# Three small early reads of x and of two weights into an unused buffer, in a kernel of cross attention and a gated MLP

## The chip, the cores and the metric

The kernel runs on one core of one Trainium2 chip. The metric is the device time in microseconds (us); the kernel before has a median of 220.04 us over 3 runs (219.81 to 221.09).

## What is computed

For each of 8 batches and 8 heads, x (512 tokens of 64 values) and a state (32 slots of 64 values) attend to each other. Both results, 544 rows per batch of 8 × 64 = 512 values, then go through a gated MLP with 1536 hidden values. Inputs and output are float32.

```
scores = scale * x @ state.T        a  = softmax(scores)    xread = a  @ state
scores2 = scale * state @ x.T       a2 = softmax(scores2)   sread = a2 @ x
t = concat([xread, sread], rows)    -> (B * 544, 512)
out = (relu(t @ w_gate) * (t @ w_val)) @ w_out
```

## The kernel before

The matrix products run in bf16. For the x rows the kernel does not build xread: it forms U = state · w (lines 291 to 320, for both weights), so that `gv` (line 338) needs only the normalised attention `ANS` as the other operand. `relu` on ScalarE (line 351) and `mult` on VectorE (line 356) make `h_sb`, and `out_part` (line 402) multiplies it with `w_out` into `o_ps`. The state rows are collected in `br` and go through the same weights at the end (`gvs`, line 343).

The order of the first third is written out by hand: the string `program` (lines 455 to 483) names every step, and each engine takes its instructions in that order. The steps that matter here:

- Ahead of the string, lines 414 to 420 issue the first loads without a cast: SP issues heads 0 and 1 of batch 0; ScalarE issues the state of batches 0 and 1 and then heads 2 and 3 of batch 0. They land in `st_f` and `xf`, and `stc` and `xc` cast them. Line 427 issues heads 4 to 7 of batch 0 from GpSimd, which casts in the transfer.
- `dx.1.0.2` and `dx.1.1.2` (line 434) load batch 1 in two halves. `dw.w.lo.n` (line 109) loads n columns of all 512 rows of a weight: 0 is gate, 1 is value. All these come from GpSimd's queue, one behind the other: four pieces of 128 columns, then ten of 256.
- `spin32` and `spin` (line 438) are matmuls of constants into an unused bank; they stand between the early steps and keep TensorE running.
- `xT` transposes x on TensorE and `xo` copies it out of PSUM; `sc` makes the scores, `ex` the exponentials, `nr` and `nx` the normalisation. `c` makes columns of U, `co` copies them, and `gv`, `re`, `mu` and `o` are the MLP.

x lies in memory as (batch, head, token, 64 values). One batch is 1 MB, one head 128 KB. A row of `w_gate` or `w_val` is 6 KB.

After these, SP issues transposes in the transfer (for example `ad.2`, line 226) and the output rows (line 379). The pool `const` is the first in the memory of a partition; behind it lie, in this order, the pools of `U`, `xf`, `xb` and the other attention tiles, small tiles, `ANS`, `h_sb`, `g_sb` and `o_sb`.

Of the kernel before, what the change touches and what calls it, by code (L numbers as in the profile page):

```python
# [8 lines left out]
FP32 = mybir.dt.float32  # L9
# [7 lines left out]
def kernel(  # L17
# [9 lines left out]
    nc = tc.nc  # L27
# [10 lines left out]
    def pool(name, bufs, space=None):  # L38
        if space is None:
            return ctx.enter_context(tc.tile_pool(name=name, bufs=bufs))  # L40
        return ctx.enter_context(tc.tile_pool(name=name, bufs=bufs, space=space))

    const = pool("const", 1)
# [53 lines left out]
    def state_dma(eng, lo, hi):  # L97
        src = state.rearrange("(g b) h (m i) d -> (b h m) g i d", b=2, i=4)
        eng.dma_start(out=st_f[:, lo // 2:hi // 2], in_=src[:, lo // 2:hi // 2])
# [312 lines left out]
    ctx.enter_context(tc.manual_schedule())  # L412
    nc.vector.memset(stT, 0.0)
    xf[0] = xin.tile([128, HK, NC, D], FP32, name="xf", tag="xf")
    for eng, j in ((nc.sync, 0), (nc.scalar, None), (nc.scalar, 1)):
        if j is None:
            state_dma(eng, 0, 2)
        else:
            src = x[0, 2 * j:2 * j + 2].rearrange("h (p c) d -> p h c d", c=NC)
            eng.dma_start(out=xf[0][:, 2 * j:2 * j + 2], in_=src)  # L420
    nc.scalar.activation(out=tiny, in_=nc.const_aps.tensor(0.0, (128, 1), FP32), func=AF.Exp)

    def w_load(w, lo, n):
# [130 lines left out]
    for g in range(first, NF * (B + 1)):  # L554
        b, jf = divmod(g, NF)
# [47 lines left out]
```

## Time and profile before

| | us |
|---|---|
| median of 3 runs | 220.04 |
| the profiled execution | 219.39 |
| its span, first to last instruction | 217.6 |
| TensorE busy (1952 matmuls) | 212.8 |
| VectorE busy | 135.0 |
| ScalarE busy | 117.8 |
| GpSimd busy | 42.5 |

The span is that of one profiled execution; 1.79 us of its 219.39 lie outside it. Matmuls overlap in the pipeline, so their durations add to more than the time they occupy. PE is the matmul part of TensorE and PEld its loading of the stationary operand; DVE is VectorE, ACT ScalarE, POOL GpSimd, SP SyncE; a q behind a name is the engine's issuing queue. In a row of the timeline the first number is the start in us from the span's start, the second the duration, and the bracket tells how long the engine was idle before and what ended that. The chain of waits follows the work that ended last back to its start. A row of the transfers gives the size and the time from the start of the issue to the landing. "DMA share" is the summed time of packets over 16 transfer engines and the length of the window: over 1 means that packets overlap on an engine. GB/s counts what is written; the casting loads read twice as many bytes as they write.

### The profile page before, as it was taken

Reading aid. Unit: us, or ns where it says so; the run is one execution under the profiler, and the core shown is the slowest. Engines: PE = TensorE matmul, PEld = TensorE weight load, DVE = VectorE, ACT = ScalarE, POOL = GpSimd, SP = SyncE. Lnnn points to the kernel's source line nnn. Section 1 sums busy time; section 2 is a strip of 40 time slices with the busy share of each in tenths; the row PEclk is TensorE's granted clock in tenths of the full one; section 3 lists DMA queues with packets and bytes.
Section 4 is the critical chain, followed back from the end, with each engine's and each line's share of the span. In section 5 each row is a group of like instructions: output and inputs, shape, how many; then the busy total and the mean of one; then the engine's idle time right before and its main releaser. Section 6 shows DMA issues by size and latency. Waiting matters only on the chain.

```text
span 217.6 us, 4865 instructions
## 1 busy us (share of the span) xinstructions
PE 212.8 (98%) x1952; PEld 104.8 (48%) x1952; DVE 135.0 (62%) x233; ACT 117.8 (54%) x225; POOL 42.5 (20%) x63
## 2 busy tenths in 40 slices
PE   8899999999999999999999999999999999999994
PEld 4554454454444444444444444444544445666543
DVE  4799967956887678557966796388745444222100
ACT  4798877747546556455555656454646443333221
POOL 7974049005600531020107000000000000000000
PEclk9999999999999999999999999999999999999999
DMA  7999999579963995919491453131311122222132
GB/s 168 180 196 197 202 221 171 78 139 188 152 175 74 144 186 110 167 52 193 99 148 60 110 134 96 49 99 50 84 28 51 48 48 50 61 56 80 51 96 96
DMA packets 47399, 24.96 MB, mean 115 GB/s; under 512 B 27824, under 2 KB 43056, under 8 KB 47376
## 3 DMA queue, kind: packets, MB, share of 16 engines
q0 software_dynamic: 16896, 9.05, 31.0%
q1 hardware_dynamic: 29584, 14.85, 28.7%
q10 hardware_dynamic: 896, 0.75, 1.3%
q8 instruction: 15, 0.25, 0.4%
q14 instruction: 8, 0.07, 0.2%
HBM read 18.35 MB, written 8.91 MB: 125 GB/s over the span
## 4 chain that ended last, share of the span: by engine, by line
PE 96%; DVE 1%; ACT 1%; issue 0%
PE o_ps L367 40%; PE gv_ps L325 38%; PE gv_ps L347 5%; PE up L298 4%; PE warm_ps L440 2%; PE upc L298 2%; PE o_ps L396 1%; PE sr_ps L265 1%; PE sc_ps L179 1%; PE sT_ps L189 1%; PE xT_ps L162 1%; ACT e_sn L206 1%; DVE xT L165 1%; ACT xT L165 0%; PE aT_ps L234 0%; DVE cs L212 0%
## 5 line engine op out<-in xcount | busy, mean ns | idle before, releaser
L367 PE MATMUL o_ps<-wo_sb,h_sb 128*128 128x512 bf16 x372 | 94.3, 379 | 0.0
L325 PE MATMUL gv_ps<-ans,U 128*128 128x512 bf16 x384 | 93.2, 379 | 0.0
L358 DVE TENSOR_TENSOR h_sb<-gv_ps,g_sb 128x512 bf16<-128x512 f32 x96 | 65.1, 688 | 42.8 <-ACT g_sb L354 41.3
L354 ACT ACTIVATE g_sb<-gv_ps 128x512 bf16<-128x512 f32 (+1 forms) x108 | 61.7, 578 | 51.4 <-PE gv_ps L325 39.1
L325 PEld LDWEIGHTS <-U 128*128 128x128 bf16 x384 | 37.1, 98 | 44.5 <-issue 0.8
L367 PEld LDWEIGHTS <-h_sb 128*128 128x128 bf16 x372 | 35.2, 98 | 42.0 <-issue 4.0
L310 DVE CAST U<-up 128x512 bf16<-128x512 f32 x44 | 27.7, 684 | 5.7 <-PE up L298 5.7
L375 ACT COPY o_sb<-o_ps 128x512 f32<-128x512 f32 x31 | 18.4, 594 | 19.7 <-PE o_ps L367 17.7
L310 ACT CAST U<-up 128x512 bf16<-128x512 f32 x28 | 14.7, 595 | 8.8 <-PE up L298 8.8
L254 POOL COPY xa<-xb 128x1024 bf16<-128x1024 bf16 x16 | 16.0, 1045 | 10.0 <-PE sr_ps L265 5.9
L358 DVE TENSOR_TENSOR hs_sb<-gv_ps,g_sb 128x256 bf16<-128x256 f32 x12 | 5.1, 425 | 15.3 <-PE gv_ps L347 10.4
L212 DVE TENSOR_REDUCE cs<-e_sn 128x16 f32<-128x512 bf16 x16 | 10.8, 677 | 1.1 <-ACT e_sn L206 1.1
L218 DVE TENSOR_TENSOR a_sn<-e_sn,rc 128x512 bf16<-128x512 bf16 x16 | 10.9, 687 | 0.4
L298 PEld LDWEIGHTS <-stT 64*32 64x32 bf16 x560 | 6.7, 91 | 6.4 <-issue 5.3
L320 ACT CAST U<-upc 128x512 bf16<-128x512 f32 (+1 forms) x19 | 8.7, 522 | 1.7 <-PE upc L298 1.7
L446 POOL COPY mark<-g_sb 128x1 bf16<-128x1 bf16 x4 | 0.8, 190 | 41.8 <-ACT g_sb L354 41.8
L197 ACT ACTIVATE eT<-sT_ps 128x512 bf16<-128x512 f32 x10 | 5.4, 594 | 5.3 <-PE sT_ps L189 5.3
L434 POOL DMA_DIRECT2D xb<-in_x_dram x8 | 6.8, 847 | 3.1 <-DMA wg_sb<-in_moe_w_gate_dram 1.4
L347 PE MATMUL gv_ps<-br,wg_sb 128*128 128x256 bf16 x48 | 7.2, 273 | 0.0
L347 PE MATMUL gv_ps<-br,wv_sb 128*128 128x256 bf16 x48 | 7.2, 273 | 0.0
L399 DVE COPY o_sb<-o_ps 128x64 f32<-128x64 f32 x2 | 0.4, 224 | 10.6 <-PE o_ps L396 10.5
L298 PE MATMUL up<-wg_sb,stT 64*32 64x512 bf16 (+1 forms) x168 | 6.9, 348 | 0.0
(59 smaller groups left out, 124.1 us busy)
## 6 DMA issues: line engine op xcount, KB each, us to landing
out_dram<-o_sb SPq DMA_DIRECT2D x26, 256.0 KB, 2.4
xb<-in_x_dram POOLq DMA_DIRECT2D x6, 512.0 KB, 7.1
wo_sb<-in_moe_w_out_dram POOLq DMA_DIRECT2D x2, 768.0 KB, 10.5
out_dram<-o_sb SPq DMA_DIRECT2D x11, 128.0 KB, 2.4
wg_sb<-in_moe_w_gate_dram POOLq DMA_DIRECT2D x5, 256.0 KB, 9.4
wv_sb<-in_moe_w_val_dram POOLq DMA_DIRECT2D x5, 256.0 KB, 10.0
xb<-in_x_dram POOLq DMA_DIRECT2D x3, 256.0 KB, 5.3
st_f<-in_state_dram POOLq DMA_DIRECT2D x1, 384.0 KB, 11.4
```

Of the source, the lines that this page charges most:

```text
L212: nc.vector.reduce_sum(out=cs, in_=e_v, axis=AX.X)
L218: {"dve": nc.vector, "pool": nc.gpsimd}[eng].tensor_tensor(out=a_sn[b][:, jp].rearrange("p c (j n) -> p c j n", n=Ns), in0=e_v, in1=held[" ...
L254: nc.gpsimd.tensor_copy(out=v[:, hs], in_=xb[b][:, hs])
L298: nc.tensor.matmul(dst[kc][i0:i0 + 32], stT[r:r + 64, parity, b, h], wsb[r:r + 64, j, lo:lo + n], start=True, stop=True)
L310: copy[eng](out=U[b][:, w, kc, lo:lo + 512], in_=held["u", b, w, lo][kc])
L320: copy[eng](out=U[b][:, :, kc, lo:lo + n], in_=held["c", b, lo][kc])
L325: nc.tensor.matmul(ps[w], U[b][:, w, kc, f0:f0 + 128], ANS[b][:, kc].rearrange("p c t -> p (c t)"), start=(kc == 0), stop=(kc == NK - 1))
L347: nc.tensor.matmul(ps[w][:, 0:nt], wsb[:, j, f0:f0 + 128], br[:, j].rearrange("p b n -> p (b n)"), start=(j == 0), stop=(j == NJ - 1))
L354: nc.scalar.activation(out=g_sb[:, 0:n], in_=ps[0][:, 0:n], func=AF.Relu)
L358: nc.vector.tensor_tensor(out=dst, in0=ps[1][:, 0:n], in1=held["g", b, jf][:, 0:n], op=ALU.mult)
L367: nc.tensor.matmul(held["o", b, tsub], src[:, jf, tsub * 128:(tsub + 1) * 128], wo_sb[:, jf], start=(jf == 0), stop=(jf == NF - 1))
L375: copy[eng](out=o_sb, in_=held["o", b, tsub])
```

## The change

Behind SP's first load (heads 0 and 1 of batch 0), and in the program's text behind ScalarE's two, SP issues three more. Each copies 32 bytes (8 float32) from the start of each of a row of equal stretches into a new tile `touch` in the pool `const`:

- of x: 96 pieces, one each 64 rows of 64 values (16 KB), from 512 KB to 2 MB, which is heads 4 to 7 of batch 0 and all of batch 1;
- of `w_gate` and of `w_val`: 32 pieces each, one each 16 rows (96 KB), over the whole weight.

Nothing reads `touch`. It takes 96 bytes of each partition at the end of `const`, so every tile of the later pools begins 96 bytes further on: `o_sb`, for example, at byte 212896 in place of 212800. Nothing else is edited, and the order on the other engines is as before.

```diff
     xf[0] = xin.tile([128, HK, NC, D], FP32, name="xf", tag="xf")
+    touch = const.tile([96, 3, 8], FP32, name="touch")
+
+    def touch_dma(k, src, lo, n, step):
+        v = src.rearrange("(a r) c -> a r c", r=step)[lo:lo + n, 0, 0:8]
+        nc.sync.dma_start(out=touch[0:n, k], in_=v)
+
     for eng, j in ((nc.sync, 0), (nc.scalar, None), (nc.scalar, 1)):
         if j is None:
             state_dma(eng, 0, 2)
         else:
             src = x[0, 2 * j:2 * j + 2].rearrange("h (p c) d -> p h c d", c=NC)
             eng.dma_start(out=xf[0][:, 2 * j:2 * j + 2], in_=src)
+    touch_dma(0, x.rearrange("b h s d -> (b h s) d"), 32, 96, 64)
+    touch_dma(1, moe_w_gate, 0, 32, 16)
+    touch_dma(2, moe_w_val, 0, 32, 16)
     nc.scalar.activation(out=tiny, in_=nc.const_aps.tensor(0.0, (128, 1), FP32), func=AF.Exp)
```

## The prediction

> **What bounds the kernel.** I read the page's busy times and slices first, then the chain of waits in order of time, then the timeline of the first 20 us beside the landings of single transfers, because the change touches only the first microseconds.
>
> ```profile
> span 217.6 us, 4865 instructions
> PE 212.8 (98%) x1952; PEld 104.8 (48%) x1952; DVE 135.0 (62%) x233; ACT 117.8 (54%) x225; POOL 42.5 (20%) x63
> ...
> DMA  7999999579963995919491453131311122222132
> ...
> PE 96%; DVE 1%; ACT 1%; issue 0%
> ```
>
> TensorE is busy 98% of the span and the chain of waits is 96% TensorE, with no transfer among its shares. The transfer engines are full in the first slices of 5.4 us each. So faster loads can help only in the opening, and only where TensorE or the chain waits for one. The chain there:
>
> ```profile
> 0.78 3.75 PE warm_ps L440 x4
> ...
> 5.17 0.44 PE xT_ps L162 x4
> ...
> 5.63 0.42 DVE xT L165
> ...
> 8.38 0.25 DVE rc L214
> ...
> 8.66 0.70 DVE xT L165
> ...
> 9.41 0.42 PE sc_ps L179 x8
> ...
> 15.91 2.70 PE gv_ps L325 x12
> 18.61 0.56 PE upc L298 x32
> ```
>
> It opens with 3.75 us of matmuls on constants, whose length no load sets. From 5.63 to about 12 us it runs through VectorE and ScalarE; from there TensorE works without a gap. Beside it stand these instructions and landings:
>
> ```profile
> 0.74 0.46 SPq L420 DMA_DIRECT2D xf<-in_x_dram  x1
> 1.19 0.45 ACTq L420 DMA_DIRECT2D xf<-in_x_dram  x1
> 2.67 1.50 POOL L434 DMA_DIRECT2D xb<-in_x_dram  x2
> 4.16 0.76 POOL L109 DMA_DIRECT2D wg_sb<-in_moe_w_gate_dram  x1
> 4.72 0.45 DVE L144 CAST xb<-xf 128x512 bf16<-128x512 f32 x1 [0.88 <-DMA xf<-in_x_dram]
> 4.89 0.77 POOL L109 DMA_DIRECT2D wv_sb<-in_moe_w_val_dram  x1
> 5.50 0.53 PE L162 MATMUL xT_ps<-id,xb 128*128 128x128 bf16 x4
> 5.62 0.78 POOL L109 DMA_DIRECT2D wg_sb<-in_moe_w_gate_dram  x1
> 6.35 0.79 POOL L109 DMA_DIRECT2D wv_sb<-in_moe_w_val_dram  x1
> 7.97 0.62 PE L162 MATMUL xT_ps<-id,xb 128*128 128x128 bf16 x8
> 9.54 0.74 POOL L109 DMA_DIRECT2D wv_sb<-in_moe_w_val_dram  x1 [0.18 <-issue]
> ```
>
> ```profile
> xf<-in_x_dram ACTq DMA_DIRECT2D x1, 256.0 KB, 3.5
> xb<-in_x_dram POOLq DMA_DIRECT2D x1, 256.0 KB, 5.2
> wg_sb<-in_moe_w_gate_dram POOLq DMA_DIRECT2D x1, 128.0 KB, 5.8
> wv_sb<-in_moe_w_val_dram POOLq DMA_DIRECT2D x1, 128.0 KB, 5.8
> wv_sb<-in_moe_w_val_dram POOLq DMA_DIRECT2D x1, 256.0 KB, 8.8
> ```
>
> The time to landing counts from the issue's start, so each load has a spare, the time by which it may be late before the chain moves:
>
> - Heads 2 and 3 of batch 0, from ScalarE's queue: 1.19 + 3.5 = 4.69. The cast ends at 4.72 + 0.45 = 5.17 and TensorE transposes at 5.50: spare 0.3 us.
> - First half of batch 1: 2.67 + 5.2 = 7.87. Its eight transposes run from 7.97 to 7.97 + 0.62 = 8.59, and VectorE, which copies them, is free at 8.38 + 0.25 = 8.63: **spare 0.04 us**, the smallest. Earlier arrival gains nothing: VectorE is the later of the two.
> - The fourth value piece: 9.54 + 8.8 = 18.34, first used by the `upc` at 18.61, to which TensorE comes without a gap: spare 0.25 us or so.
>
> **The change, part by part.** *Three issues on SP.* One issue of SP's takes 0.46 us (the row at 0.74), so they fill SP from 1.20 to about 2.6 us. What is queued behind them:
>
> ```profile
> SPq L226 <- DVE sn L274: 43.1, 1, 43.1
> ```
>
> SP then waits 43.1 us for VectorE before its next issue, so this costs nothing; without that cover it would be 3 × 0.46 = 1.4 us. Nobody waits for the new transfers. Each transfer on SP's and ScalarE's queues waits, for its counter, for the eighth transfer before it; three more shift which counter it is but not that distance, so I take nothing for it.
>
> *160 pieces on the transfer engines.* They are 96 + 32 + 32 reads of 32 bytes, 10 on each of 16 engines if spread evenly. They come behind SP's own load in its queue and meet ScalarE's load and the first casting loads of GpSimd. The trace has no 32-byte read. The nearest row is the 128-column weight pieces: 512 runs of 256 bytes written each, landing at 4.16 + 5.8 = 9.96 and 4.89 + 5.8 = 10.69. That is 0.73 us for 512 runs on full engines, so 160 runs hold the stream 0.73 × 160 / 512 = **0.23 us**. (GpSimd also issues them 0.73 us apart, so the engines alone may do them faster.) The ends of this term come from a queue's total and from an idle stretch:
>
> ```profile
> q0 software_dynamic: 16896, 9.05, 31.0%
> ```
>
> ```profile
> 2.00:3.00 1.00, 1.00 (x2) 0.43 (x2) 1.00 (x1) 0.99 (x2) 0.93 (x4) 1.00 0.79 223
> 8.00:9.00 1.00, 1.00 (x17) 0.78 (x17) 0.93 (x3) 0.62 (x3) 1.00 (x2) 1.00 1.60 171
> 9.00:10.00 1.00, 0.74 (x16) 0.59 (x16) 1.00 (x3) 0.72 (x2) 0.82 (x2) 1.00 1.81 178
> 10.00:11.00 1.00, 0.91 (x23) 0.44 (x20) 0.93 (x3) 1.00 (x2) 1.00 (x2) 1.00 1.82 179
> 12.00:13.00 1.00, 0.96 (x53) 0.59 (x50) 0.97 (x4) 1.00 (x3) 1.00 (x2) 1.00 1.45 195
> ```
>
> A packet of GpSimd's queue (q0) takes 31.0% × 16 × 217.6 us / 16896 = 64 ns. Ten of them without overlap are 0.64 us, the upper end. The lower end of the cost is 0: the share of 0.79 from 2 to 3 us leaves some engine time free, and the pieces may fall there.
>
> The Trainium skill speaks against the change here, in "DMA: Bandwidth & Descriptors", section "Measured (HBM→SBUF, 128 partitions, SWDGE, issued from GpSimd)": it puts the floor of a small transfer at about 10.5 ns for each packet. By that, an estimate, 160 pieces would hold the engines 1.7 us, and the sum below would be +1.6 in place of +0.2. The rows above show 512 runs in 0.73 us, 1.4 ns each, on full engines, so the trace does not bear this floor out for runs of 256 bytes; no run here shows it for 32.
>
> *What the reads may save.* If the first read of a stretch is slow, the loads behind the touches run faster. The window rows bound this: from 8 to 11 us, when new stretches of x and of both weights are first read, 171, 178 and 179 GB/s are written against 195 at 12 to 13 us. The deficit is 24 + 17 + 16 = 57 KB, and 57 KB / 195 GB/s = 0.29 us. Most of that I put to the 512-byte reads of the narrow pieces, because the second pair of narrow pieces, over the same rows, shows the same 0.73 us: issued at 5.62 and 6.35, with the same 5.8 us to landing. I take a saving of 0, with 0.29 us as its end.
>
> *What arrives late, and the sum.* The stream behind the touches is late by 0.23 us (−0.29 to +0.64). ScalarE's load eats that in its spare of 0.3. Batch 1's first half has 0.04: the copy at 8.66, the scores at 9.41 and all behind them move 0.23 − 0.04 = 0.19 us. The fourth value piece moves 0.23 against a TensorE that comes 0.19 later, inside its spare. TensorE is full from then on, so what is lost stays lost. Sum: 219.39 + 0.19 = 219.58 for the profiled execution. The median of the runs shown is 0.65 above that execution, so 220.04 + 0.19 = **220.2 us**.
>
> *The shift of 96 bytes* of every later tile costs nothing that a row shows. Only a slower matmul would move the end. I take 0.
>
> **The rivals.**
>
> 1. *Nothing was cold, and the pieces fit into idle engine time.* For it: share 0.79 from 2 to 3 us. Against: the share is 1 and above from 3 us on, and SP's own load stands ahead of the pieces. The time stays at 220.0.
> 2. *The loads land sooner, and that helps.* The end of the saving is 0.29 us. Against: no link of the chain is a transfer, and VectorE at 8.63 is later than the data. For it: timed runs are 0.65 us above the profiled one, so there a load may be the later. Then 220.04 − 0.29 = 219.75; with all 0.65 recovered, 219.4.
> 3. *The pieces themselves pay a slow first read, with engines held.* This one ends on the slow side, and its price comes from the first load against a late transfer of the same size:
>
> ```profile
> xf<-in_x_dram SPq DMA_DIRECT2D x1, 256.0 KB, 3.3
> ...
> out_dram<-o_sb SPq DMA_DIRECT2D x1, 256.0 KB, 2.0
> ```
>
>    The first took 1.3 us longer (part of that is other traffic, and one reads while the other writes). If one such wait holds the engines for all pieces together, the chain moves 1.3 − 0.04 = 1.26 us: 221.3. If each of the three transfers pays it, 3.9 − 0.04: 223.9. It passes 1% when the pieces hold the engines 2.2 us, 0.22 us for each of the ten on an engine. Against: 0.73 us for 512 first-read runs of a weight leaves no room for many such waits.
> 4. *The 96-byte shift slows reads.* The price is by the two large groups of matmuls:
>
> ```profile
> L367 PE MATMUL o_ps<-wo_sb,h_sb 128*128 128x512 bf16 x372 | 94.3, 379 | 0.0
> L325 PE MATMUL gv_ps<-ans,U 128*128 128x512 bf16 x384 | 93.2, 379 | 0.0
> ```
>
>    They are 756, so one nanosecond on each is 0.76 us, 220.8. Nothing in the trace speaks for it.
>
> **How the numbers follow.** My forecast, a small loss from the pieces (220.05 to 220.6), has 0.45; no change 0.22; a small gain 0.15; the slow first reads 0.12, a third of it with each transfer paying; the shift 0.06. The predicted time is that of the forecast, 220.2. The range goes from 219.4 (all of the saving in rival 2) to 221.3 (one slow wait in rival 3), which leaves out the 223.9 and some tails, under 2 in 10. The bound of 1%, 2.2 us, is about what a measurement of this kernel can tell from no change. No case gains 2.2 us, so faster gets 0.02 for what I have not seen; slower has the bad third of rival 3 and a little of rival 4, 0.06; within 1% is 0.92.
>
> **What would show it.** Right: SP's three issues between 1.2 and 2.6 us; the first half of batch 1 landing near 8.1 in place of 7.87; the copy of its transposes by VectorE near 8.85 in place of 8.66, waiting for TensorE; the matmuls at 18.61 near 18.8; everything later moved by as much. Rival 1 would show the same landing as now, rival 2 an earlier one and 9 to 11 us at 190 GB/s or more. Rival 3 would show landings late by 1 us and a gap on TensorE between 5.5 and 9 us. The shift would show in a mean matmul time above 379 ns. I am wrong if the landing moves by more than 0.64 us or if the time falls while the chain's opening stays as it is.

## The result

| | us | runs |
|---|---|---|
| before, median | 220.41 (219.51 to 221.92) | 22 |
| changed, median | 219.56 (219.00 to 220.94) | 22 |
| ratio | 0.9969, 95% interval 0.9956 to 0.9983 | |
| profiled execution, before / changed | 219.39 / 219.64 | |

The changed kernel is 0.31% faster, some 0.7 us by the ratio and 0.85 between the medians, where 0.19 us of loss was forecast. The time lies in the range of 219.4 to 221.3, and the sign is the other one. At the same time its profiled execution is slower than the profiled one of before. The page after:

```profile
span 217.8 us, 4845 instructions
PE 209.6 (96%) x1926; PEld 104.3 (48%) x1952; DVE 134.8 (62%) x233; ACT 117.9 (54%) x225; POOL 42.6 (20%) x63
```

TensorE's record count fell from 1952 to 1926 while its weight loads stand at 1952: matmul records are missing, so its 209.6 us are no gain. What the opening looks like, first the timeline of the changed kernel (start, duration, instruction):

```profile
1.25 0.45 SPq L419 DMA_DIRECT2D touch<-in_x_dram  x1
1.75 0.43 SPq L419 DMA_DIRECT2D touch<-in_moe_w_gate_dram  x1
2.22 0.42 SPq L419 DMA_DIRECT2D touch<-in_moe_w_val_dram  x1
8.41 0.62 PE L162 MATMUL xT_ps<-id,xb 128*128 128x128 bf16 x8 [0.30 <-DMA xb<-in_x_dram]
9.06 0.69 DVE L165 COPY xT<-xT_ps 128x1024 bf16<-128x1024 bf16 x1 [0.65 <-PE xT_ps L162]
11.81 0.38 PE L179 MATMUL sc_ps<-stT,xT 128*128 128x64 bf16 x7
```

Then its landings; the last row is the first half of batch 1, issued at 2.67:

```profile
touch<-in_x_dram SPq DMA_DIRECT2D x1, 3.0 KB, 3.5
touch<-in_moe_w_gate_dram SPq DMA_DIRECT2D x1, 1.0 KB, 5.1
touch<-in_moe_w_val_dram SPq DMA_DIRECT2D x1, 1.0 KB, 4.8
xb<-in_x_dram POOLq DMA_DIRECT2D x1, 256.0 KB, 5.7
```

It lands at 2.67 + 5.7 = 8.37 in place of 7.87 (these rows give the way to the landing to 0.1 us; the trace's own records have 8.36 and 7.92, which is 0.44 later). VectorE waits 0.65 us for the transposes of it, and the third scores start at 11.81. In before they did so at

```profile
11.41 0.41 PE L179 MATMUL sc_ps<-stT,xT 128*128 128x64 bf16 x8
```

so the opening lost 0.40 us, yet the spans as the pages round them differ by 0.2. The way of the loss is the one that the prediction names, 0.44 less a spare of 0.04. But the chain of waits of the changed kernel goes through another load, the first value piece:

```profile
4.98 6.22 DMA wv_sb<-in_moe_w_val_dram
11.19 0.04 issue
11.24 0.25 PE upc L298 x8
11.48 0.32 PE warm_ps L449
11.81 0.01 issue
11.81 0.41 PE sc_ps L179 x8
```

The two ways end together here: ScalarE's copy of the transposes, which the scores also need, ends at 11.76. From the third scores to ScalarE's last two output issues (their rows stand under "The end") both kernels take the same time, 214.16 − 11.41 = 202.75 us and 214.56 − 11.81 = 202.75 us. So between these two profiles only the opening and the end differ.

Something gave 0.2 us back, and the timed runs gave more. Two rows of the wait lists of SP near the end, before and after, hold the first hint:

```profile
SPq L598 <- DMA out_dram<-o_sb: 1.4, 2, 1.1
```

```profile
SPq L607 <- DMA out_dram<-o_sb: 1.2, 4, 0.6
```

The same waits at the kernel's last line are 1.4 us in 2 pieces before and 1.2 us in 4 pieces after.

### The profile page after: what moved, and what is told of

Read it like the earlier page. It is cut to its first block, busy times and chain, and to the rows that moved or that the text cites. A ratio compares the mean times of both kernels' runs of the same rounds, so it can differ in the third digit from the quotient of the medians.

```text
span 217.8 us, 4845 instructions
## 1 busy us (share of the span) xinstructions
PE 209.6 (96%) x1926; PEld 104.3 (48%) x1952; DVE 134.8 (62%) x233; ACT 117.9 (54%) x225; POOL 42.6 (20%) x63
## 4 chain that ended last, share of the span: by engine, by line
PE 92%; DMA 3%; issue 2%; POOL 1%; DVE 0%; POOLq 0%
PE o_ps L367 39%; PE gv_ps L325 38%; PE gv_ps L347 5%; PE up L298 4%; DMA wv_sb<-in_moe_w_val_dram 3%; PE upc L298 2%; PE o_ps L396 1%; PE sr_ps L265 1%; PE sT_ps L189 1%; POOL xb L443 1%; PE sc_ps L179 0%; PE aT_ps L234 0%; PE xT_ps L162 0%; POOL wg_sb L109 0%; PE warm_ps L449 0%
## 5 line engine op out<-in xcount | busy, mean ns | idle before, releaser
L367 PE MATMUL o_ps<-wo_sb,h_sb 128*128 128x512 bf16 x354 | 90.6, 379 | 2.4 <-issue 2.2
L358 DVE TENSOR_TENSOR hs_sb<-gv_ps,g_sb 128x256 bf16<-128x256 f32 x12 | 5.1, 425 | 15.3 <-PE gv_ps L347 10.4
L399 DVE COPY o_sb<-o_ps 128x64 f32<-128x64 f32 x2 | 0.5, 225 | 10.6 <-PE o_ps L396 10.5
```

The costliest lines, as they stand in the source:

```text
L358: nc.vector.tensor_tensor(out=dst, in0=ps[1][:, 0:n], in1=held["g", b, jf][:, 0:n], op=ALU.mult)
L367: nc.tensor.matmul(held["o", b, tsub], src[:, jf, tsub * 128:(tsub + 1) * 128], wo_sb[:, jf], start=(jf == 0), stop=(jf == NF - 1))
```

## The experiments

Each ratio is to the kernel before, run on the same chip in turns.

**The shift of the tiles alone.** One 32-byte read of head 0, in place of the three.

```diff
-    touch_dma(0, ...); touch_dma(1, ...); touch_dma(2, ...)
+    nc.sync.dma_start(out=touch[0:1, 0], in_=x[0, 0, 0:1, 0:8])
```

> The unused tile stays, so all later tiles still begin 96 bytes further on, and SP issues one read of 32 bytes of head 0 of batch 0, which its own load reads anyway, in place of the three. If the shift of the tiles is the cause, the time is that of the changed kernel, 0.9969 of before (some 0.7 us less). If the early reads of new stretches are the cause, it is that of before: ratio 0.999 to 1.001.

Measured: 219.86 us, 0.999 (0.9975 to 1.0005). The interval leaves out the 0.9969 of the changed kernel, so the shift does not carry that gain. It is too wide to part small effects.

**The same pieces from rows already read.**

```diff
-    touch_dma(0, x.rearrange("b h s d -> (b h s) d"), 32, 96, 64)
-    touch_dma(1, moe_w_gate, 0, 32, 16)
-    touch_dma(2, moe_w_val, 0, 32, 16)
+    rows = x.rearrange("b h s d -> (b h s) d")
+    touch_dma(0, rows, 0, 96, 8)
+    touch_dma(1, rows, 96, 32, 8)
+    touch_dma(2, rows, 96, 32, 8)
```

> The same three transfers of 96, 32 and 32 pieces of 32 bytes, but all from heads 0 and 1 of batch 0, which SP's load ahead of them reads. If the gain comes from reading each later stretch once ahead of its load, nothing is gained and the pieces only cost: 1.000 to 1.002 (0 to 0.4 us more). If the traffic itself gives the gain (by delaying or spreading the loads behind it), or the order of the counters does, the ratio stays 0.997.

Measured: 219.79 us, 0.9995 (0.9977 to 1.0012), so beside 0.9969 most of the gain is not in the traffic. Its profiled execution, of span 219.2, shows a loss of another kind. In this row of its timeline TensorE waits for the value columns 256 to 511:

```profile
17.13 0.30 PE L298 MATMUL upc<-wv_sb,stT 64*32 64x256 bf16 x8 [1.05 <-DMA wv_sb<-in_moe_w_val_dram]
```

In before the same matmuls start without a wait, at 15.40. In the window from 14.9 to 16.1 us one packet of the instruction queue shares the engines:

```profile
q8 instruction: 1, 0.02, 4.7%
```

That is 4.7% × 16 × 1.2 us = 0.9 us of one engine. It became theory A below: that a weight piece meets this packet and comes late. But before has the same packet, from 14.5 to 15.7 us, and nothing is late there:

```profile
q8 instruction: 1, 0.02, 4.9%
```

By the traces' records it runs in all 20 profiles, from a start at 14.2 to 15.3 us, and the piece is late in two of them.

**Only the pieces of x; only those of the weights** (the other lines left out).

> Only the 96 pieces of x; the weights are first read by their loads. If slow first reads are the cause and fall mostly on the second half of batch 0 and on batch 1, most of the gain stays: 0.9975. If they fall on the weights, 1.000. My guess by the smallest spare (0.04 us, batch 1) is that x carries the larger part: 0.998.

> Only the 64 pieces of the two weights. If the first narrow pieces of the weights are what comes late in the timed runs of before, 0.997 to 0.998; if x is, 1.000. If the two parts add, the shortfalls of this and of the kernel with the pieces of x alone sum to 0.0031.

Measured: 219.89, 0.9985 (0.9972 to 0.9999), and 219.82, 0.9987 (0.9973 to 1.0002). Only the first interval lies below 1, and neither part is clearly the larger. The shift alone has the same number of extra transfers as the pieces of x alone and ran beside them: 219.86 against 219.89, so the pieces of x alone show no gain of their own.

**Before against itself, and the changed kernel again.**

> The kernel before, unchanged, against itself: ratio 1.000, and its interval shows what a difference between equal kernels looks like. Its profile is a second execution of before: if the first one (span 217.6) was a lucky one, the first half of batch 1 lands later here than at 7.87 us, by 0.2 to 0.8, and the span is 218 or more; if the first was typical, the opening is the same to 0.05 us.

> The changed kernel, unchanged, once more, on the same chip as the others of this batch. If the early reads save first reads whatever the chip, 0.997 to 0.9985; if the gain was that of one chip, 0.999 to 1.001. Its profile should again show its opening within 0.1 us of the first one's (scores at 11.81), if the reads make the opening steadier.

Measured: 1.000 (0.999 to 1.001) and 0.9987 (0.9975 to 0.9999). The gain is there on a second chip, 0.3 us by the ratio and 0.4 by the medians. The changed kernel's opening is not as steady as was expected: in this profile the scores start at 11.64, in the first at 11.81. The new profile of before answers a question of the prediction. Its chain has, in order of time:

```profile
2.68 5.47 DMA xb<-in_x_dram
8.14 0.05 issue
8.19 0.64 PE xT_ps L162 x8
8.83 0.02 issue
8.85 0.70 DVE xT L165
...
11.60 0.41 PE sc_ps L179 x8
```

Here the first half of batch 1 *is* a link of the chain: it lands 0.2 us later than in the first profile (8.14 against 7.92 by the records), and the scores start at 11.60. The first profile of before was an early case.

**Fewer pieces**, over the same stretch of memory (the diff in short form).

```diff
-    touch_dma(0, ..., 32, 96, 64);  (gate and value) 0, 32, 16
+    touch_dma(0, ..., 1, 3, 2048);  (gate and value) 0, 4, 128     # few
+    touch_dma(0, ..., 8, 24, 256);  (gate and value) 0, 8, 64      # quarter
```

> 3 pieces of x (one each 512 KB) and 4 of each weight (one each 768 KB) in place of 96 and 32. If what is slow is the first read of a large stretch (half a MB or more), the whole gain stays, with less traffic: the same ratio as the changed kernel run beside it, or up to 0.001 less. If stretches are small (16 KB of x, 96 KB of weight), most first reads stay in the loads: 0.999 to 1.000.

> 24 pieces of x (one each 64 KB) and 8 of each weight (one each 384 KB), a quarter of the pieces. If stretches of 64 KB or more matter, the same ratio as the changed kernel beside it. If they are smaller than 64 KB, between it and before. If the number of pieces itself costs time, less than the changed kernel by 0.0005 or so (0.17 us by the price of the prediction for the 120 pieces left out).

Measured: 219.65, 0.9991 (0.998 to 1.0002), and 219.69, 0.999 (0.9979 to 1.0001), beside 0.9987 of the full number. The intervals overlap; how large a stretch is can't be read from them.

**The weights later or earlier** (theory A, and theory B, by which only the opening up to 12 us matters). `late` loads 64 gate columns once more, into a place where nothing reads them; `early` leaves out the load of value columns 128 to 255, and VectorE writes zeros there.

```diff
-    dw.0.0.128 dw.1.0.128 dw.0.128.128 dw.1.128.128 dw.0.256.256
+    dw.0.0.128 dw.1.0.128 dw.0.128.128 dw.1.128.128 late dw.0.256.256   # late
+    dw.0.0.128 dw.1.0.128 dw.0.128.128 dw.0.256.256                     # early
```

> Before, with one more piece of weight (64 gate columns once more, into a place that nothing reads) ahead of the first 256-column piece: every later weight lands some 0.5 us later. Theory A: in the timed runs of before the value piece of columns 256 to 511 lands sometimes before and sometimes behind TensorE's first use of it (15.40 us in the first profile, spare 0.5), and when it meets the 16 KB read of the instruction queue at about 14.6 to 15.0 us it comes 1.2 us late, as in the profile with the same-place pieces. Then nearly all runs now lose 0.7 to 1.3 us: ratio 1.004, and the profile shows that wait at 15 to 17 us. Theory B: only the opening up to 12 us matters (batch 1's first half). Then this extra load, behind it in the queue, costs at most 0.1 us: 1.000.

> The changed kernel with the same extra piece. Theory A: it loses too, 1.003 to 1.004, and what the early reads save on the weights is no longer enough. Theory B: it stays at the changed kernel's 0.9985.

> Before without the load of value columns 128 to 255 (zeros stand there instead), so each later weight is issued and lands about 0.7 us earlier. Theory A: the late cases vanish and the time falls as with the early reads or more: 0.997 to 0.9985. Theory B: 0.9995 to 1.000, since batch 1 is ahead of the piece left out.

> The changed kernel without that piece. Theory A: the early reads have nothing left to save and only their cost stays, so it is equal to or above the one without them (its ratio 0.000 to 0.001 higher). Theory B: the early reads still give their 0.0013 over before.

Measured: 1.0013 (0.9996 to 1.0031), 1.0022 (0.9998 to 1.0045), 0.9998 (0.9986 to 1.0011) and 0.9974 (0.9958 to 0.999). The profiled execution of before with `late` has the same wait at the same matmuls:

```profile
17.28 0.30 PE L298 MATMUL upc<-wv_sb,stT 64*32 64x256 bf16 x8 [1.17 <-DMA wv_sb<-in_moe_w_val_dram]
```

So the late case is not one kernel's alone, but it is not what the gain is made of: with the weights 0.7 us earlier before gains nothing, and the changed kernel keeps its gain. Theory A falls as the main cause. Theory B does not fit all four either. With the weights later it expected the changed kernel at 0.9985, which the interval of 0.9998 to 1.0045 leaves out: it is then no faster than before with the same piece (220.21 against 220.12). Why the gain is not seen there stays open. The end of the kernel was the next place to look.

**The end.** The three new transfers take part in a rotation: each transfer of SP and ScalarE counts on the next of 8 counters. At the end of the program SP waits for counter 0, then 1, up to 7, one instruction each. The last transfer, an output piece of ScalarE, counts on 1 in before and on 4 in the changed kernel. In before six waits stand behind the one that it releases, in the changed kernel three. Six or eight extra transfers put it on 7, or back on 1:

```diff
-    touch_dma(0, ...); touch_dma(1, ...); touch_dma(2, ...)   # six, eight: no early reads
+    for k in range(6):                                     # or 8
+        nc.sync.dma_start(out=touch[32 + k:33 + k, 1], in_=x[0, 0, k:k + 1, 0:8])
```

The other two keep the three lines and add 3 or 5 such reads behind them.

> No early reads of new stretches; in their place SP issues six reads of 32 bytes of head 0 of batch 0. Theory C: part of the gain comes at the end. SP's last waits go through the 8 transfer counters in the order 0 to 7; the last output transfer counts on 1 in before, on 4 in the changed kernel, and here on 7, so six waits behind it become waits ahead of it. From the profiles three such steps are 0.18 us (the time from the last matmuls to the end of the span), so six are 0.36 us: ratio 0.9984, and in its profile the tail from the last output issue to the end is 0.36 us shorter than in before. Theory D (the gain is all in the first reads): 1.000.

> Eight such reads, so the last output transfer counts on 1 again as in before. Theory C: 1.000, tail as in before. If the shift of the tiles or the small traffic had made the tail shorter, it would be as short here as with three or more: 0.9985 or less.

> The changed kernel with three more small reads, six transfers in all: early reads of new stretches and the last counter on 7. If both parts hold, it is the fastest: the gain of six (0.0016) plus that of the early reads alone (0.0005 to 0.001): 0.9975 to 0.998. If the early reads give nothing, equal to the kernel with six.

> The changed kernel with five more small reads, eight in all: the early reads without the change at the end. It measures the early reads alone. Theory D: 0.997 to 0.9985 as in the two runs of the changed kernel. Theory C alone: 1.000. Both: 0.9990 to 0.9995.

| | last counter | us | ratio |
|---|---|---|---|
| eight, no early reads | 1 | 219.92 | 0.9995 (0.9975 to 1.0015) |
| early reads, eight in all | 1 | 219.87 | 0.9992 (0.9973 to 1.001) |
| six, no early reads | 7 | 219.74 | 0.9989 (0.9967 to 1.0011) |
| early reads, six in all | 7 | 219.61 | 0.9973 (0.9952 to 0.9995) |

By times alone the four hardly part. Their profiles do. For each kernel, here is the start of ScalarE's last two output issues; first before (its span is 217.6), then the changed kernel (217.8), whose waits of SP stand above:

```profile
214.16 1.02 ACTq L400 DMA_DIRECT2D out_dram<-o_sb  x2
```

```profile
214.56 1.02 ACTq L400 DMA_DIRECT2D out_dram<-o_sb  x2
```

Then six (span 217.9), its timeline and its waits of SP:

```profile
214.83 1.02 ACTq L400 DMA_DIRECT2D out_dram<-o_sb  x2
```

```profile
SPq L606 <- DMA out_dram<-o_sb: 0.9, 3, 0.3
```

And eight (span 217.6), the same two:

```profile
214.12 1.02 ACTq L400 DMA_DIRECT2D out_dram<-o_sb  x2
```

```profile
SPq L606 <- DMA out_dram<-o_sb: 1.4, 2, 1.1
```

From that issue to the end of the span are 3.46 us in before, 3.28 in the changed kernel, 3.07 with six and 3.45 with eight (with the spans of the traces' records, 217.62, 217.84, 217.90 and 217.57). SP's waits go the same way: 1.4, 1.2, 0.9 and again 1.4 us. The records of SP's single instructions, which no view above prints, show the cause. In before the last output lands at 216.31, the wait that it releases ends at 216.36, and six more waits end one after another up to 216.73, 0.06 us apart. In the changed kernel it lands at 216.73, the wait that it releases ends at 216.77, and three more end up to 216.95. With six, none is left. The same output takes its time, but fewer waits follow it. Theory C holds for the end: it goes with the counter and returns with eight, whatever is read (3.44 us with early reads and eight in all).

**The early reads alone, with the same end.** A quarter of the pieces and three small reads, beside six small reads:

```diff
+    for k in range(3):        # behind the quarter's three lines
+        nc.sync.dma_start(out=touch[32 + k:33 + k, 1], in_=x[0, 0, k:k + 1, 0:8])
```

> The early reads with a quarter of the pieces (24 of x, 8 of each weight) and three small reads, six transfers in all, so the last counter is 7. If the early reads save time of their own beside the end, this is 0.0005 to 0.0013 below the kernel with six small reads alone, run beside it, near 0.9975. If they save nothing, both are at 0.9985.

> The kernel with six small reads of head 0 and no early reads, once more: the end alone. By the 0.39 us that its profile shows at the end, 0.9982 against before; in its first run 0.9989.

Measured: 219.32, 0.9965 (0.9952 to 0.9978), and 219.64, 0.9982 (0.997 to 0.9995). In this run six small reads without any early read are clearly faster than before, by the 0.4 us of the end (0.0018 × 220); in their first run, 0.9989, that was not clear. The quarter with six has the lowest time and ratio of all kernels here; against the changed kernel itself (0.9969 and 0.9987 on other chips) it was not run side by side.

The two profiles of the kernel with six small reads also show how far the opening moves from one execution to the next. The third scores have these rows in their chains, first run and second:

```profile
12.09 0.41 PE sc_ps L179 x8
```

```profile
11.53 0.35 PE sc_ps L179 x8
```

That is half a microsecond between two executions of the same kernel, more than the 0.40 us between the first profiles of before and of the changed kernel.

## Why the prediction was wrong

**Bounds and the path of the delay: right in the first pair of profiles, but the delay is not shown to be that of the pieces.** SP's issues stand at 1.25 to 2.64 us, hide behind its long wait and hold nobody. In that pair the first half of batch 1 comes 0.44 us later, not 0.23, and the delay goes through VectorE's copy into the scores, which move by 0.40. Against the second profile of before (scores at 11.60) it is 0.21, and from there to the second of the changed kernel (11.64) 0.04. Over the seven profiles with all 160 pieces this load lands at 8.04 to 8.45, on average at 8.24. Over the eight without the pieces it lands at 7.54 to 8.63, on average at 8.16. So the term of 0.23 us is not borne out: what the pieces cost, if anything, is lost between executions. The prediction also gave no spare to the first value piece, through which the chain of the changed kernel goes.

**The step that failed first** is a term set to nothing: "three more shift which counter it is but not that distance, so I take nothing for it." The distance to the eighth transfer before is indeed the same. What the step overlooked is the end, where the counters are waited for in a fixed order and the last transfer's place in that order is not free to ignore. Three more transfers save 0.2 us there, six 0.4, eight nothing, by the tails above, and every profile agrees: the tail is 3.43 to 3.47 us with no extra transfer or with eight, 3.37 with one or two, 3.25 to 3.30 with three, 3.07 to 3.10 with six. With this term the sum of the prediction's own numbers is 0.19 − 0.2, about 0: no loss, and not yet 0.7 of gain.

**The second failure is the base.** "Earlier arrival gains nothing: VectorE is the later of the two" rested on one execution, and a spare of 0.04 us cannot be read from one. That execution was early among its kind: 219.39 us, where the 22 runs beside the changed kernel have 219.51 as their lowest (single runs on other chips reached 219.04). The prediction noted the 0.65 us between it and the median, and moved the sum up by it instead of asking which loads are late in the runs that it did not see. In the second profile of before the load is a link, so an earlier arrival can gain there: rival 2, given 0.15, was nearest to what came (219.4 to 219.75). That it was, and that the time lies in the range at all, is partly luck: a part of the gain is the end, which neither holds, and the landings that should come sooner by rival 2 do not (8.24 against 8.16 above).

**What the early reads themselves save stays open in size.** Three pairs of kernels share the end and differ in the reads: 219.87 against 219.92, 219.61 against 219.74, 219.32 against 219.64 (each pair on one chip). A fourth, without the value piece, has 219.54 against 220.00, of which the end explains 0.2. That is 0.05, 0.13, 0.32 and about 0.26 us to one side, none far outside its noise; by the means of the runs the four together give 0.25 us, 95% of about 0.1 to 0.4, an estimate made after the fact. Two more pairs do not join them: the pieces of x alone against the shift alone (219.89 against 219.86), and the two kernels with `late` (220.21 against 220.12). On the first chip 0.85 us lie between the medians, and the end explains 0.2 of that. What slow first reads cost there was not measured, and no profile of a changed kernel shows an opening earlier than the first one of before. That the reads make late loads rarer fits, and is argued, not shown. One count speaks for it, made after the fact: apart from the kernels with `late`, 28 of the 266 timed runs without early reads took more than 220.5 us, and 1 of the 122 with them; the end explains some of this. The written rate gives the prediction's bound of 0.29 us little: from 8 to 9 us it rose from 171 to 180 GB/s, from 9 to 11 us it is 179 against 178 and 179 before,

```profile
8.00:9.00 1.00, 0.70 (x14) 0.60 (x14) 0.38 (x2) 0.78 (x2) 1.00 (x2) 1.00 1.69 180
9.00:10.00 1.00, 0.45 (x16) 0.36 (x14) 0.94 (x2) 0.60 (x1) 0.46 (x2) 1.00 1.80 179
10.00:11.00 1.00, 1.00 (x25) 0.66 (x22) 0.97 (x3) 0.74 (x2) 1.00 (x2) 1.00 1.81 179
```

so from 9 us on the early reads did not lift it. That the lower rate belongs to the narrow pieces, as the prediction took it, fits but was not tried.

**The rivals.** Nothing but idle time (1): the time did not stay, though for the opening alone the landings above do not exclude it. Pieces holding the engines for more than 2.2 us (3): they landed 3.5 to 5.1 us after their issue, but the load behind them moved by 0.4, not by 1.3. The floor of 10.5 ns for each packet that the Trainium skill gives in "DMA: Bandwidth & Descriptors", section "Measured (HBM→SBUF, 128 partitions, SWDGE, issued from GpSimd)", would have cost 1.7 us, an estimate that the 0.4 us do not bear out. The shift (4): its own kernel was 0.999 (0.9975 to 1.0005), the 202.75 us between opening and end are the same with and without it, and the large matmuls still take 379 ns:

```profile
L367 PE MATMUL o_ps<-wo_sb,h_sb 128*128 128x512 bf16 x354 | 90.6, 379 | 2.4 <-issue 2.2
L325 PE MATMUL gv_ps<-ans,U 128*128 128x512 bf16 x377 | 92.5, 379 | 0.3
```

## What to carry to other kernels

A change that adds or removes a transfer also moves the last transfer to another counter; where the end of the program waits for the counters in order, that alone is worth tenths of a microsecond, and small reads at a cheap place can choose it. Before a spare of a few hundredths is used, look at a second execution: one profile shows one arrival of each load. And an effect of 0.1 to 0.3% wants its control with the same number of transfers, or the control's own end is taken for the effect.

## What the runs showed of the hardware

- A wait of SP on a counter that is already full costs about 0.06 us: in before six of them end between 216.36 and 216.73.
- One load can take much longer in one execution than in the others. The value columns 256 to 511 landed 6.6 to 7.8 us after the start of their issue in 18 profiles and after 9.3 and 8.5 us in two, where they held TensorE 1.05 and 1.17 us. A 16 KB packet of the instruction queue took about 0.9 us of one transfer engine beside them. As it also ran in the 18 others, it is not enough as a cause, and that queue is not the kernel's to move.
- 160 reads of 32 bytes, 5 KB in all, took 3.5 to 5.1 us to land, and 3.4 to 4.0 in the second profile, which is longer than the 3.3 us of the 256 KB load that SP issued ahead of them.
